# Where GpSimd computes the low part of the attention output, and where the two row maxima of a score tile lie

## The chip, the cores and the metric

The kernel is one program on one core of a Trainium2 chip. The metric is the device time of one execution in microseconds. Before the change three runs took 513.75, 514.60 and 514.68 us; the median is 514.6 us. Engine names are those of the profile: PE is the matrix engine (PEld its weight loads), DVE is VectorE, ACT is ScalarE, POOL is GpSimd, SP is the engine that issues the DMAs.

## The reference

Causal attention over 2 batches, 12 heads, 448 positions and 64 dimensions feeds a gated projection, which feeds a second projection with a SoLU and a layer norm. All matrices are float32.

```
scores = q k^T / sqrt(64), masked above the diagonal
attn   = exp(scores - max(scores)) / (sum + 1e-9)
x      = attn v                      -> 896 tokens x 768
x      = (sigmoid(x w_gate) * (x w_val)) w_out       (768 -> 1536 -> 768)
h      = x w_in;  s = h * softmax(h);  out = layernorm(s) * g  w_out2   (768 -> 1024 -> 768)
```

## The kernel before

Each float32 operand is split into a high part that the matrix engine takes as it is and a low part (the operand minus its high part), and products are made from three terms: high x high, high x low, low x high. So every tensor that reaches PE has a "hi" instruction and a "lo" instruction.

The attention stage works on 12 pairs of heads. A table of steps, `STEPS` (lines 486 to 501), lists every operation with a step number and an engine; pair p does an operation of number s0 in step 8p + s0. In each step the loop at line 510 writes out, in this order, PE's operations, ACT's, DVE's and POOL's, and within an engine those of one step stand in the order of the table. So the table alone sets the order of each engine's instructions, and up to four pairs are under way at once. Each engine runs its own list in order and waits on semaphores.

The names that the change and the prediction use, with the step number in brackets:

- `sc_mm` (0 and 4; lines 319 to 339): the scores of a pair, in two groups of query tiles (448 + 64 keys, then 320 + 192 keys), into a PSUM tile `s`. The second group is the one that line L338 shows as 64x320.
- `sc_max` (0, 1, 4, 5; DVE, L351): the negated row maxima of a query tile for both heads of the pair, two numbers per partition, into columns 8 to 15 of a small tile `sum`. A maximum is named here by the columns that it reads over both heads: 896, 640, 384 or 128.
- `sc_exp` (1, 2, 5, 6; ACT, L358): exponentials with the maximum as bias, the row sums into columns 0 to 7 of `sum`.
- `sums` (7, POOL, L363, tile `rs`), `recips` (8, DVE, L367): the sums and their reciprocals. `rs_wide` (8, POOL, L374 through the helper at L221, tile `rx`): the reciprocals spread to 64 columns for each head. `rs_mm` (10, PE, L381, tile `r`): `rx` transposed on PE.
- `tr_mm`, `tr_hi`, `tr_lo` (from 9 on; PE L409, ACT L416, DVE L229, tiles `t` and `pt`): the exponentials transposed and split. `pv_mm` (13 to 20, PE L441): the products with v, tile `x`.
- `x_mul`, `x_hi`, `x_lo` (21, 22, 23; DVE L447, ACT L219, POOL L456 through L229; tiles `xf` and `xy`): the product times the reciprocals, and its two parts.
- for later pairs: `prep_k_hi` and `prep_q_hi` (-7 and -6, POOL L221 and L234), `prep_k_lo` (-5, DVE L229) and `prep_q_lo` (-2, DVE L249), all into `qks`; `prep_v_hi` and `prep_v_lo` (7 and 9, POOL L221 and L229, tile `v`); `last_keys` (3, POOL L221, tile `p`).

After the attention, from about 129.5 us on, come the matmuls of the two projections, with their weights streamed in and split.

Of the kernel before, what the change touches and what calls it, by code (L numbers as in the profile page):

```python
# [16 lines left out]
AX = mybir.AxisListType  # L17
PSUM = bass.MemoryType.PSUM

B, H, S, D = 2, 12, 448, 64  # L20
# [3 lines left out]
NQ = 4  # L24
# [20 lines left out]
def attn_moe_moe2(ctx: ExitStack, tc: tile.TileContext, qk, v, w_gv, w_out, w_in2, w_out2, g_ln, out):  # L45
# [3 lines left out]
    nc = tc.nc  # L49
# [140 lines left out]
    with ExitStack() as actx:  # L190
# [35 lines left out]
        ENG = dict(rx='P', qh='P', kh='P', kl='D', vh='P', vl='P', xh='A', xl='P', rr='A', lk='P')  # L226
# [65 lines left out]
        sum_t = [one.tile([128, 16], F32, name=f"sum{i}") for i in range(3)]  # L292
# [11 lines left out]
        ps = ps_x.tile([128, S], F32, tag="x", name="warm")  # L304
# [34 lines left out]
                                         rhs=t[rows, ck, :n], start=False, stop=(m == 2), skip_group_check=True)  # L339

        def sums_of(p, i, e):
            k = NQ * (1 - e) + i
            return sum_t[p % 3][:, k:k + 1], sum_t[p % 3][:, 8 + k:9 + k]

        def sc_max(p, i):
            ps = ps_sc[p, i]
            if p == 0 and i == GROUPS[0][0]:
                for e in range(2):
                    nc.vector.reduce_max(out=sums_of(p, i, e)[1], in_=ps[:, 1 - e], axis=AX.X, negate=True)
            else:  # L350
                nc.vector.reduce_max(out=sum_t[p % 3][:, 8 + i:16:NQ], in_=ps, axis=AX.X, negate=True)  # L351

        def sc_exp(p, i):
            n = QE[i]
            ps = ps_sc.pop((p, i))
            for e in range(2):
                sm, mx = sums_of(p, i, e)
                nc.scalar.activation(out=p_t[(2 * p + e) % NPB][:, POFF[i]:POFF[i] + n], in_=ps[:, 1 - e], func=AF.Exp,  # L358
                                     bias=mx, scale=1.0, accum_out=sm)
# [101 lines left out]
        def early_tiles():  # L461
# [31 lines left out]
            (-7, ENG['kh'], prep_k_hi), (-6, ENG['qh'], prep_q_hi), (-5, ENG['kl'], prep_k_lo), (-2, 'D', prep_q_lo),  # L493
            (3, ENG['lk'], last_keys), (7, ENG['vh'], prep_v_hi), (9, ENG['vl'], prep_v_lo),
            (7, 'P', sums), (8, 'D', recips), (8, ENG['rx'], rs_wide), (11, ENG['rr'], rs_out),
            (21, 'D', x_mul), (22, ENG['xh'], x_hi), (23, ENG['xl'], x_lo),
            (1, 'A', lambda p: sc_exp(p, 3)), (2, 'A', lambda p: sc_exp(p, 0)),
            (5, 'A', lambda p: sc_exp(p, 2)), (6, 'A', lambda p: sc_exp(p, 1)),
            (0, 'D', lambda p: sc_max(p, 3)), (1, 'D', lambda p: sc_max(p, 0)),
            (4, 'D', lambda p: sc_max(p, 2)), (5, 'D', lambda p: sc_max(p, 1)),  # L500
        )

# [7 lines left out]
        for s in range(PER * NPR + 26):  # L510
# [12 lines left out]
            for c in range(2 * NE + 2):  # L523
                e = s - 88 - 9 * c
# [32 lines left out]
    with tc.tile_pool(name="psg", bufs=8, space=PSUM, reuse_waits="tile") as psg:  # L557
        for t in range(NF):
            bs = (1,) if t < NE else (0, 1)
            ps = {}  # L560
# [29 lines left out]
    for m in range(NK):  # L590
        pm = php.tile([128, B, 512], F32, tag="h", name="pm")
        ps = [pm[:, b, :S] for b in range(B)]
# [170 lines left out]
```

## Time and profile before

| what | us |
|---|---|
| median of three runs | 514.6 |
| the three runs | 513.75 to 514.68 |
| span of the profiled execution, first to last instruction | 512.5 |
| PE busy in it | 501.2 |
| attention stage, to the first matmul of the gated projection | 129.5 |
| distance from one pair's `rs` to the next one's, pairs 2 to 9 | 8.7 |

The profile is of one execution, on the one core. Its span is what the instructions cover; a run's time holds some 2 us more that lie around the span. Times below are counted from the start of the span.

### The profile page before, as it was taken

The numbers are of one execution on the slowest core, as the hardware profiler recorded it, in microseconds if no ns is written. First come the engines' busy times: TensorE is split into PE (matmuls) and PEld (weight loads), VectorE is DVE, ScalarE is ACT, GpSimd is POOL, SyncE is SP. The second block draws the span as 40 slices with busy tenths as digits, with TensorE's granted clock in tenths as the row PEclk, the third lists the DMA queues.
The fourth block names the chain that finished last, engine by engine and source line by source line (L and its number), as shares of the span: only waits on it lengthen the run. The fifth ranks groups of instructions, "written<-read, shape, count | busy, mean of one in ns | idle before, by whom it ended". The sixth has DMA issues, their size and how long they took to land.

```text
span 512.5 us, 7699 instructions
## 1 busy us (share of the span) xinstructions
PE 501.2 (98%) x2980; PEld 457.1 (89%) x2980; DVE 335.9 (66%) x512; ACT 226.4 (44%) x481; POOL 118.0 (23%) x203
## 2 busy tenths in 40 slices
PE   8899999989999999999999999999999999999997
PEld 8888888878899999999999999999998888899997
DVE  4578787887655777887777766766753887841210
ACT  4677777784532454345434432343324242432211
POOL 3375757552000000000000000000050587710000
PEclk9899999999999999999999999999999999999999
DMA  5632323112333154355433532354440221000101
GB/s 150 184 92 77 92 79 93 42 49 76 125 123 99 66 165 164 125 163 161 137 116 125 182 123 68 139 165 164 133 176 1 86 100 62 0 32 33 61 32 61
DMA packets 13204, 52.79 MB, mean 103 GB/s; under 512 B 1776, under 2 KB 2288, under 8 KB 13168
## 3 DMA queue, kind: packets, MB, share of 16 engines
q1 hardware_dynamic: 13168, 52.31, 31.4%
q8 instruction: 23, 0.38, 0.3%
q14 instruction: 13, 0.11, 0.1%
HBM read 49.55 MB, written 2.75 MB: 102 GB/s over the span
## 4 chain that ended last, share of the span: by engine, by line
PE 81%; DVE 6%; ACT 6%; POOL 5%; issue 1%; POOLq 0%; ACTq 0%
PE gv L574 33%; PE pm L604 17%; PE po L695 12%; PE h L634 11%; ACT p L358 4%; DVE sum L351 4%; POOL v L229 2%; DVE qks L229 2%; PE gv L473 1%; PE warm L308 1%; POOL rx L221 1%; PE tp L677 1%; PE x L441 1%; PE s L338 1%; PE t L409 1%
## 5 line engine op out<-in xcount | busy, mean ns | idle before, releaser
L574 PE MATMUL gv<-xy,hl 128*128 128x448 f32 x828 | 168.1, 365 | 0.6 <-ACT pre L478 0.6
L574 PEld LDWEIGHTS gv<-xy,hl 128*128 128x128 f32 x828 | 155.5, 188 | 13.2 <-ACT pre L478 1.0
L604 PE MATMUL pm<-g,hl 128*128 128x448 f32 x432 | 87.7, 365 | 0.0
L604 PEld LDWEIGHTS pm<-g,hl 128*128 128x128 f32 x432 | 81.2, 188 | 6.4
L621 POOL TENSOR_SCALAR t<-t,g_sb 128x768 f32<-128x768 f32 x8 | 9.0, 1123 | 248.1 <-PE pm L604 248.1
L134 DVE TENSOR_TENSOR hl<-t,hl 128x768 fp32r<-128x768 f32 x36 | 35.1, 975 | 40.2 <-ACT hl L131 38.4
L695 PE MATMUL po<-wo,lt 128*128 128x384 f32 x336 | 60.7, 340 | 0.0
L634 PE MATMUL h<-wi,xy 128*128 128x512 f32 x252 | 59.2, 395 | 0.0
L695 PEld LDWEIGHTS po<-wo,lt 128*128 128x128 f32 x336 | 58.7, 188 | 0.2 <-POOL wo L626 0.2
L358 ACT ACTIVATE p<-s,sum 128x448 f32<-128x448 f32 (+3 forms) x96 | 45.0, 478 | 29.9 <-DVE sum L351 14.9
L634 PEld LDWEIGHTS h<-wi,xy 128*128 128x128 f32 x252 | 47.2, 188 | 11.4
L120 DVE SCALAR_TENSOR_TENSOR t<-raw,t 128x768 int32<-128x768 int32 (+1 forms) x56 | 53.0, 946 | 1.7
L117 DVE SCALAR_TENSOR_TENSOR t<-raw,t 128x768 int32<-128x768 int32 (+1 forms) x56 | 52.6, 939 | 1.8
L441 PE MATMUL x<-pt,v 128*128 128x320 f32 (+3 forms) x252 | 53.5, 327 | 0.0
L112 ACT ACTIVATE raw<-raw 128x768 f32<-128x768 f32 (+1 forms) x56 | 47.9, 866 | 10.3 <-DMA raw<-in_wo_dram 6.0
L351 DVE TENSOR_REDUCE sum<-s 128x2 f32<-128x128 f32 (+3 forms) x47 | 31.6, 672 | 15.2 <-ACT p L358 13.4
L441 PEld LDWEIGHTS x<-pt,v 128*128 128x128 f32 x252 | 38.1, 190 | 2.0
L229 DVE TENSOR_TENSOR pt<-t,pt 128x512 fp32r<-128x512 f32 (+1 forms) x48 | 31.9, 667 | 3.8 <-ACT pt L416 3.8
L115 DVE TENSOR_SCALAR t<-raw 128x768 int32<-128x768 int32 (+1 forms) x56 | 30.6, 547 | 4.9 <-ACT raw L112 4.9
L171 DVE TENSOR_TENSOR lt<-tp,lt 128x512 fp32r<-128x512 f32 x14 | 9.7, 690 | 36.4 <-ACT lt L170 36.4
L131 ACT CAST hl<-t 128x768 fp32r<-128x768 f32 x36 | 30.0, 832 | 4.6 <-PE pm L604 4.2
L179 ACT ACTIVATE wk<-gv 128x448 f32<-128x448 f32 x23 | 11.3, 542 | 43.1 <-PE gv L574 43.1
(90 smaller groups left out, 542.7 us busy)
## 6 DMA issues: line engine op xcount, KB each, us to landing
raw<-in_gv_dram SPq DMA_DIRECT2D x24, 768.0 KB, 4.4
raw<-in_wo_dram SPq DMA_DIRECT2D x20, 768.0 KB, 4.3
raw<-in_wi_dram SPq DMA_DIRECT2D x12, 512.0 KB, 3.5
qkr<-in_qk_dram SPq DMA_DIRECT2D x22, 224.0 KB, 3.5
vr<-in_v_dram SPq DMA_DIRECT2D x12, 256.0 KB, 2.6
out_dram<-o SPq DMA_DIRECT2D x6, 384.0 KB, 2.3
qkr<-in_qk_dram SPq DMA_DIRECT2D x4, 112.0 KB, 2.7
out_dram<-o SPq DMA_DIRECT2D x2, 192.0 KB, 1.8
```

The source lines that it names most:

```text
L112: nc.scalar.activation(out=w1.bitcast(F32), in_=w1.bitcast(F32), func=AF.Copy, scale=2.0 ** -112)
L117: nc.vector.scalar_tensor_tensor(out=tt, in0=w1, scalar=-2 ** 31, in1=tt, op0=ALU.bitwise_and, op1=ALU.bitwise_or)
L120: nc.vector.scalar_tensor_tensor(out=tt, in0=w0, scalar=29, in1=tt, op0=ALU.logical_shift_right, op1=ALU.bitwise_or)
L134: nc.vector.tensor_tensor(out=lo, in0=t_t.pop(it), in1=f32(hi), op=ALU.subtract)
L229: (nc.gpsimd if eng == 'P' else nc.vector).tensor_tensor(out=out, in0=a, in1=b, op=ALU.subtract)
L351: nc.vector.reduce_max(out=sum_t[p % 3][:, 8 + i:16:NQ], in_=ps, axis=AX.X, negate=True)
L358: nc.scalar.activation(out=p_t[(2 * p + e) % NPB][:, POFF[i]:POFF[i] + n], in_=ps[:, 1 - e], func=AF.Exp, bias=mx, scale=1.0, accum_out=sm)
L441: nc.tensor.matmul(out=ps[:, 128 * j:], lhsT=l, rhs=pt_t[h][:, c, u, c0:c0 + S - 128 * j], start=(chunk == 0 and n == 0), stop=(chunk == 7 ...
L574: nc.tensor.matmul(out=ps[i, b], lhsT=w[:, a, cs], rhs=xy[kk][:, x, b * S:(b + 1) * S], start=(kk == 0 and a == 0 and x == 0), stop=(kk == ...
L604: nc.tensor.matmul(out=ps[b], lhsT=w[:, a, cs], rhs=g_t[kk][:, x, b * S:(b + 1) * S], start=(kk == 0 and a == 0 and x == 0), stop=(kk == N ...
L634: nc.tensor.matmul(out=h[:, n * 512:(n + 1) * 512], lhsT=xy[kk][:, a, tk], rhs=wi[n * NK + kk][:, c], start=(kk == 0 and i == 0), stop=(kk ...
L695: nc.tensor.matmul(out=ps[n], lhsT=lts[k // 4][:, a, k % 4], rhs=wo[k][:, c, cs], start=(k == 0 and i == 0), stop=(k == NF2 - 1 and i == 2))
```

## The change

The two maxima of a query tile, which lay four columns apart in `sum` (columns 8 + i and 12 + i), come to lie side by side (columns 8 + 2i and 9 + 2i). And `x_lo` gets step number 24 instead of 23. In a step whose number leaves 0 when divided by 8 the table has `rs_wide` ahead of `x_lo`, so on POOL the low part of pair p - 2 now stands behind the widened reciprocals of pair p.

```diff
         def sums_of(p, i, e):
-            k = NQ * (1 - e) + i
-            return sum_t[p % 3][:, k:k + 1], sum_t[p % 3][:, 8 + k:9 + k]
+            k, m = NQ * (1 - e) + i, 8 + 2 * i + (1 - e)
+            return sum_t[p % 3][:, k:k + 1], sum_t[p % 3][:, m:m + 1]
...
-                nc.vector.reduce_max(out=sum_t[p % 3][:, 8 + i:16:NQ], in_=ps, axis=AX.X, negate=True)
+                nc.vector.reduce_max(out=sum_t[p % 3][:, 8 + 2 * i:10 + 2 * i], in_=ps, axis=AX.X, negate=True)
...
-            (21, 'D', x_mul), (22, ENG['xh'], x_hi), (23, ENG['xl'], x_lo),
+            (21, 'D', x_mul), (22, ENG['xh'], x_hi), (24, ENG['xl'], x_lo),
```

POOL's list, at the first pair that has an `x_lo` beside it (pair 2; `rs` are the sums, `rx` the widened reciprocals, `xy` the output's low part, `qks` the next keys, `v` the values):

```order
 L221 TENSOR_SCALAR v_0_140<-vr_116 128x128 [waits PE_49]
 L363 TENSOR_SCALAR rs<-sum_144 128x8 [waits Activation_49]
-L229 TENSOR_TENSOR xy_75<-xf,xy_75 128x448 [waits DVE_49]
-L221 TENSOR_SCALAR rx<-rs 128x512 [waits DVE_49]
+L221 TENSOR_SCALAR rx<-rs 128x512 [waits DVE_49]
+L229 TENSOR_TENSOR xy_75<-xf,xy_75 128x448
 L221 TENSOR_SCALAR qks<-qkr 128x448 [waits DMAHW7_49,DMAHW0_49]
 L229 TENSOR_TENSOR v_0_138<-vr_116,v_0_138 128x3x2x64 [waits Pool_49]
```

The same two rows change places at pairs 2 to 11, ten times; the `x_lo` of the last two pairs stand alone, as before. The wait that `xy` had is covered by the later one of `rx`.

DVE's list is the same before and after, waits included. Here is one pair of it in the changed kernel (the reciprocal, the maximum of 896 columns, then two low parts `pt`, the low part of the keys `qks`, and the maximum of 640 columns, which waits for PE):

```order
L367 RECIPROCAL rs<-rs 128x8 [waits Pool_49]
L351 TENSOR_REDUCE sum_143<-s 128x2 [waits PE_49]
L229 TENSOR_TENSOR pt<-t,pt 128x512 [waits Activation_49]
L351 TENSOR_REDUCE sum_143<-s 128x2 [waits Activation_49]
L229 TENSOR_TENSOR pt<-t,pt 128x512 [waits DVE_49,Activation_49]
L229 TENSOR_TENSOR qks<-qkr,qks 128x448 [waits DMAHW3_49,DMAHW2_49,Pool_49]
L351 TENSOR_REDUCE sum_143<-s 128x2 [waits PE_49]
```

The second maximum (128 columns) waits for ACT, with neighbouring columns as with distant ones. PE's and ACT's lists are the same too.

## Rows read from the trace of the kernel before

**Rows 1.** The page's first part: PE's busy time, its share, its instructions.

```profile
PE 501.2 (98%) x2980; PEld 457.1 (89%) x2980; DVE 335.9 (66%) x512; ACT 226.4 (44%) x481; POOL 118.0 (23%) x203
```

**Rows 2.** Busy time by stretch (one pair; the projections): PE, PEld, DVE, ACT, POOL, granted clock, DMA.

```profile
59.30:68.04 8.74, 8.59 (x84) 7.58 (x80) 7.19 (x12) 6.64 (x23) 5.69 (x10) 1.00 0.32 84
129.50:512.50 383.00, 379.72 (x1904) 348.81 (x1904) 237.07 (x335) 137.99 (x204) 47.41 (x73) 1.00 0.32 107
```

**Rows 3.** The chain that ended last, one pair: start, us, what.

```profile
59.30 0.26 POOL rs L363
...
63.30 0.98 DVE qks L229
64.28 0.82 DVE sum L351
```

**Rows 4.** Timeline of PE, same pair: start, us, instruction, [idle before <-releaser].

```profile
60.39 0.51 PEld L441 LDWEIGHTS x<-pt,v 128*128 128x128 f32 x3
61.42 0.14 PEld L381 LDWEIGHTS r<-identx,rx 128*128 128x128 f32 x1 [0.53 <-POOL rx L221]
...
61.80 0.14 PEld L409 LDWEIGHTS t<-identx,p 128*128 128x128 f32 x1
...
63.20 1.02 PE L338 MATMUL s<-qks 64*128 64x320 f32 x12
```

**Rows 5.** Timeline of DVE, same pair.

```profile
59.71 1.04 DVE L351 TENSOR_REDUCE sum<-s 128x2 f32<-128x896 f32 x1
60.67 0.68 DVE L229 TENSOR_TENSOR pt<-t,pt 128x512 fp32r<-128x512 f32 x1
...
63.30 0.98 DVE L229 TENSOR_TENSOR qks<-qkr,qks 128x448 fp32r<-128x448 f32 x1
...
64.26 0.83 DVE L351 TENSOR_REDUCE sum<-s 128x2 f32<-128x640 f32 x1
```

**Rows 6.** Timeline of POOL, same pair.

```profile
59.64 1.14 POOL L229 TENSOR_TENSOR xy<-xf,xy 128x448 fp32r<-128x448 f32 x1
...
60.75 0.62 POOL L221 TENSOR_SCALAR rx<-rs 128x512 f32<-128x512 f32 x1
...
61.33 0.57 POOL L221 TENSOR_SCALAR qks<-qkr 128x448 fp32r<-128x448 f32 x1
...
61.86 1.42 POOL L229 TENSOR_TENSOR v<-vr,v 128x384 fp32r<-128x384 f32 x2
...
63.24 0.57 POOL L234 TENSOR_SCALAR qks<-qkr 128x448 fp32r<-128x448 f32 x1
```

**Rows 7.** Timeline of pair 1, which has no `x_lo` beside it.

```profile
24.64 0.26 POOL L363 TENSOR_SCALAR rs<-sum 128x8 f32<-128x8 f32 x1 [4.91 <-ACT p L358]
25.22 0.62 POOL L221 TENSOR_SCALAR rx<-rs 128x512 f32<-128x512 f32 x1 [0.32 <-DVE rs L367]
...
28.66 0.62 DVE L229 TENSOR_TENSOR qks<-qkr,qks 128x448 fp32r<-128x448 f32 x1
```

**Rows 8.** All DVE instructions of L229 on `qks`: ns min/median/max, first and last start.

```profile
L229 DVE TENSOR_TENSOR qks<-qkr,qks x12: 614/978/987, 4.8 to 98.2; 128x448 fp32r<-128x448 f32 x12
```

**Rows 9.** Timelines of the last two pairs, 10 and 11.

```profile
104.97 1.42 POOL L229 TENSOR_TENSOR v<-vr,v 128x384 fp32r<-128x384 f32 x2
106.06 0.75 DVE L115 TENSOR_SCALAR t<-raw 128x768 int32<-128x768 int32 x1
...
107.90 0.83 DVE L351 TENSOR_REDUCE sum<-s 128x2 f32<-128x640 f32 x1 [0.50 <-PE s L338]
...
112.55 1.15 POOL L229 TENSOR_TENSOR xy<-xf,xy 128x448 fp32r<-128x448 f32 x1
112.95 1.56 DVE L134 TENSOR_TENSOR hl<-t,hl 128x768 fp32r<-128x768 f32 x1 [0.24 <-ACT hl L131]
113.66 1.33 POOL L221 TENSOR_SCALAR rx<-rs 128x512 f32<-128x512 f32 x1
...
115.05 0.33 PE L381 MATMUL r<-identx,rx 128*128 128x128 f32 x1 [0.55 <-POOL rx L221]
```

## The prediction, written before the changed kernel ran

> **What bounds the kernel now.** I read the busy times first [rows 1], then the stretches [rows 2], then the chain that ended last [rows 3], then the timelines of one pair, engine by engine [rows 4 to 6].
>
> The busy share points at PE, with 98% [rows 1], and for the projections that is right: from 129.5 us on PE is busy for 379.7 of 383.0 us at the full clock [rows 2]. The change touches nothing there, so that part only starts earlier or later. In the attention stage PE's share is as high, but its weight loads fill only 7.58 of 8.74 us, and DVE, ACT and POOL have idle time too [rows 2]. No engine is full; a loop over engines sets the length of a pair. The chain goes round it: sums on POOL at 59.30, low part of the keys on DVE at 63.30, maximum of 640 columns at 64.28 [rows 3], then exponentials on ACT, and the next pair's sums 8.74 us after the first, at 68.04 [rows 2].
>
> The chain has only one predecessor at each step, so I ask what else that maximum waits for. By the order of DVE it waits for PE's scores. These end at 63.20 + 1.02 = 64.22, and the maximum starts at 64.26 [rows 4, 5]. On DVE, an instruction that waits for nothing starts some 0.08 before the recorded end of the one in front (at 60.67, where the maximum of 896 columns ends at 59.71 + 1.04 = 60.75 [rows 5]). The low part of the keys ends at 64.28 [rows 5], so without the wait for PE the maximum would have started at 64.20. Two paths thus end within 0.06 us of each other:
>
> - PE's: POOL does x's low part from 59.64 and only then the widened reciprocals from 60.75 [rows 6]. PE is through with the loads in front at 60.39 + 0.51 = 60.90, stands idle for 0.53 us and begins their transposes at 61.42 [rows 4]. All that stands behind in its queue is late, the scores too.
> - DVE's: the low part of the keys lasts 0.98 us [rows 5], where the shortest of its kind takes 0.61 [rows 8]. POOL's high part of the queries runs from 63.24 to 63.81 [rows 6], and the low part ends 0.47 us after that. The same instruction takes 0.62 us in pair 1, where no x_lo delays POOL [rows 7]. So it is being held up by POOL, and goes on when that POOL instruction is over.
>
> **The change part by part.** Two neighbouring columns instead of distant ones: 47 maxima with two results each. Reading 640 columns takes 0.83 us [rows 5], 1.3 ns each, so two results are worth 2.6 ns; between a gain and a loss of that size, 47 x 2.6 ns = 0.1 us either way. I take 0. No wait goes with it, as DVE's list shows.
>
> The swap on POOL, ten times. x_lo is one instruction with no DMA in it, and the widened reciprocals are all that it is moved past. In the pair with its sums at T: now x_lo starts at T + 0.34, rx at T + 1.45, the next keys at T + 2.03, v's low part at T + 2.56, the queries' high part at T + 3.94 [rows 3, 6]. Changed, rx has to wait for the reciprocal: in pair 1, which has that order, it starts 0.58 after the sums [rows 7]. It keeps POOL 0.58 (60.75 to 61.33) and x_lo 1.11 (59.64 to 60.75) [rows 6], so x_lo starts at T + 1.16, the keys at T + 2.27, v's low part at T + 2.80 with its end at T + 4.22, the queries at T + 4.18. All that stands behind the swap comes 0.24 later, since POOL idles for the reciprocal. The keys' high part is still done long before T + 4.00, when DVE wants it.
>
> PE's path: rx is ready at T + 1.2 instead of T + 2.07, before PE arrives (60.90 is T + 1.60), so the idle 0.53 goes. What is late next: the transposes behind it reuse a PSUM tile that DVE's low part `pt` frees at 60.67 + 0.68 = 61.35 [rows 5]; with 0.04 for the signal they move from 61.80 [rows 4] to about 61.39. The gain on this path is 0.41: scores end at T + 4.51.
>
> DVE's path: the keys' low part still arrives at T + 4.00. Then POOL is in v's low part, to T + 4.22. If DVE goes on as soon as that is over, it ends at 4.22 + 0.47 = T + 4.69, where now it is T + 4.98, and the queries' high part waits for DVE instead. That POOL lets DVE in between two instructions that stand back to back is seen in pair 11: DVE's hl, which began at 112.95 behind x_lo (to 113.70), ended at 114.51, 0.81 after x_lo, while rx, queued right behind, took 1.33 us for its usual 0.62 [rows 6, 9]. The maximum can start at T + 4.69 - 0.08 = T + 4.61; it was T + 4.96. Gain 0.35, and this is the later of the two paths. From the other side: if POOL's hold ended a little later, 0.30; if the low part met no hold at all, PE's path would decide, 0.41.
>
> The Trainium skill (Perfetto Trace Analysis, GPSIMD Instruction) says not to trust the reported span of a GpSimd instruction and to use the spacing of starts. By that rule v's low part is over when the queries' high part starts, at T + 4.18, the keys' low part ends at T + 4.65, and eight pairs give 0.3 us more than the sum below. I keep the ends, since DVE's hl ended at the time that they give.
>
> This pattern stands in pairs 2 to 9, eight times: the median of the keys' low part over the run is 978 ns [rows 8]. From the maximum to the next sums nothing changes: ACT and DVE work by turns there, and PE and POOL, both earlier or idle, are not waited for. Eight pairs: 8 x 0.35 = 2.8 us.
>
> Pair 10 has no keys to prepare. There the maximum waits 0.50 for PE alone [rows 9]. PE gains 0.41 as above, to 107.49. But v's low part on POOL ends 0.24 later, at 106.63 instead of 106.39, and DVE's L115, which ends 0.42 after it now (106.81), ends at 107.05; the low part behind it ends 0.6 later, and the maximum can start at about 107.54. Gain 0.36.
>
> Pair 11: rx starts 0.24 after x_lo's present start, at 112.79, and is over at 113.41. PE, idle for 0.55 before 115.05 [rows 9], can start the transposes at 114.50. DVE's hl, which PE needs next, ends 0.81 after rx, at 114.22, in time. Gain 0.55; x_lo then waits for hl, and v's low part comes later, but PE needs it only four steps on.
>
> The sum: 2.8 + 0.36 + 0.55 = 3.7 us. The span becomes 508.8 instead of 512.5; the median of the runs stands 2.1 us above the span, which I keep: 514.6 - 3.7 = 510.9 us.
>
> **The rivals.**
>
> *POOL keeps its turn (slower).* If POOL's next instruction gets ahead of the waiting DVE, the keys' low part waits for the queries' high part as now, but that ends at T + 4.18 + 0.57 = T + 4.75. The low part ends at T + 5.22, the maximum starts at T + 5.14, 0.18 later than now: 8 x 0.18 = 1.4 us lost. In pair 11 hl would wait for x_lo as well, and the 0.55 goes; pair 10 keeps its 0.36. Sum 1.1 us slower, 515.7. For it: now, too, the low part waits for exactly this POOL instruction, which starts 0.06 ahead of it [rows 5, 6]. Against: pair 11, where DVE came in between. It decides once the queries' high part starts reading before DVE is let in. The Trainium skill (SBUF — State Buffer, SBUF: two separate sides) has it that of the two engines the one that starts first holds the shared ports for its whole instruction, which also puts the waiting low part first; the starts in rows 5 and 6 agree so far.
>
> *Only PE's wait goes.* If the keys' low part ends where it does now, because its 0.98 us is not POOL's doing, the maximum can start at 64.20 instead of 64.26: 8 x 0.06 + 0.36 + 0.55 = 1.4 us, 513.2. For it: 0.98 us is the same in eight pairs. Against: 0.62 us in pair 1 [rows 7].
>
> *Nothing.* PE's queue is in order, and what it gains at one wait it may lose at the next, for `pt` or for the queries' parts that now come later: 514.6. For it: PE's slack is small, its weight loads alone take 7.58 of 8.74 us [rows 2]. Against: the path behind the wait is followed above to the maximum.
>
> **How the numbers follow.** The forecast gets 0.70, the slower rival 0.08, the wait alone 0.12, nothing 0.10. The forecast's own range: eight pairs at 0.30 to 0.41 (2.4 to 3.3), pair 10 at 0.2 to 0.5, pair 11 at 0.3 to 0.9, so 2.9 to 4.7 us, 509.9 to 511.7. Half a microsecond is what the three runs differ by to either side. To hold 8 in 10 the range reaches to the wait alone, 509.7 to 513.3, and leaves out nothing and slower. A measurement here tells 0.2%, 1 us, from no change. Faster by more: the forecast and two thirds of the wait alone, 0.78. Within: the rest of that and nothing, 0.14. Slower by more: 0.08.
>
> **What would show it.** In the changed profile rx starts 0.58 after the sums in every pair, and the idle time of PE before L381 is gone in pairs 2 to 11. The keys' low part lasts some 0.69 us instead of 0.98, and the queries' high part is the one drawn out, to about 0.9. The sums follow each other after 8.37 us in place of 8.72. If they come 8.9 apart and the keys' low part lasts 1.2, POOL kept its turn. If PE's idle time turns up before L409 or L338 instead, it is nothing. If the low part gets short and the distance stays, the loop is another one than mine, and the prediction is wrong in its first part.

## The result, and the profile after

| | before | after |
|---|---|---|
| median of the runs, us | 514.64 | 510.40 |
| the runs, us | 513.75 to 514.90 | 509.67 to 510.87 |
| span of the profiled execution, us | 512.5 | 507.9 |
| `rs` to `rs`, pairs 2 to 10, mean us | 8.73 | 8.40 |
| `rs` of pair 10 to `rs` of pair 11, us | 9.29 | 8.89 |
| `rs` of pair 11 to the first matmul of the gated projection, us | 17.28 | 16.51 |

The ratio of the times is 0.9918, with a 95% interval of 0.9904 to 0.9932: 4.2 us faster. Forecast were 510.9 us and a gain of 3.7.

The trace says where the gain lies. From the first pair that has an `x_lo` beside it (pair 2) to the projections it is 8 x 0.33 = 2.6 us in the pairs, 0.4 us in pair 10 and 0.8 us in pair 11, together 3.8 us. The projections last as long as before. The other 0.85 us between the two spans stands ahead of pair 2, where the change moves nothing: the `rs` of pair 2 starts at 33.13 and 32.28 us. In the kernels run for this study that moment lies anywhere from 32.1 to 33.7 us. What differs there is PE's granted clock, as one stretch shows (columns: start and end, length, then busy time of PE, PEld, DVE, ACT and POOL, granted clock as a share of full speed, DMA share, GB/s). Before, with a mean of 0.67, so in part at the lower of the two levels (1.2 of 2.4 GHz):

```profile
17.00:20.00 3.00, 3.00 (x25) 2.88 (x23) 1.09 (x3) 2.16 (x10) 2.57 (x6) 0.67 0.98 274
```

After, at the full clock:

```profile
17.00:20.00 3.00, 3.00 (x38) 2.86 (x35) 1.41 (x4) 2.81 (x11) 2.83 (x6) 1.00 0.93 263
```

The kernel before itself runs in both ways: of its 18 executions beside the first set of experiments, those with a mean clock of 1.000 have spans of 511.6 to 511.8 us and those with 0.997 spans of 512.1 to 513.0 us. So the comparison below goes by distances within the stage and not by spans.

One pair after, to be laid beside [rows 4 to 6]. Its sums `rs` start at T = 57.48 us; for [rows 4 to 6] T was 59.30. POOL first (timeline: start, us, instruction, and in brackets the idle time before it and what ended it):

```profile
57.48 0.25 POOL L363 TENSOR_SCALAR rs<-sum 128x8 f32<-128x8 f32 x1 [2.08 <-ACT p L358]
58.06 0.62 POOL L221 TENSOR_SCALAR rx<-rs 128x512 f32<-128x512 f32 x1 [0.32 <-DVE rs L367]
58.64 1.15 POOL L229 TENSOR_TENSOR xy<-xf,xy 128x448 fp32r<-128x448 f32 x1
59.76 0.57 POOL L221 TENSOR_SCALAR qks<-qkr 128x448 fp32r<-128x448 f32 x1
60.29 1.43 POOL L229 TENSOR_TENSOR v<-vr,v 128x384 fp32r<-128x384 f32 x2
61.69 0.94 POOL L234 TENSOR_SCALAR qks<-qkr 128x448 fp32r<-128x448 f32 x1
```

The widened reciprocals start at T + 0.58, x's low part behind them, and the queries' high part at T + 4.21 lasts 0.94 us, where it was 0.57. PE in the same pair:

```profile
58.52 0.50 PEld L441 LDWEIGHTS x<-pt,v 128*128 128x128 f32 x3
59.03 0.14 PEld L381 LDWEIGHTS r<-identx,rx 128*128 128x128 f32 x1
59.64 0.14 PEld L409 LDWEIGHTS t<-identx,p 128*128 128x128 f32 x1
...
60.99 1.02 PE L338 MATMUL s<-qks 64*128 64x320 f32 x12
```

The row of L381 has no bracket any more: PE goes from one load to the next. Its scores end at 62.01, T + 4.53. DVE in the same pair:

```profile
58.85 0.68 DVE L229 TENSOR_TENSOR pt<-t,pt 128x512 fp32r<-128x512 f32 x1
...
61.48 0.72 DVE L229 TENSOR_TENSOR qks<-qkr,qks 128x448 fp32r<-128x448 f32 x1
...
62.13 0.81 DVE L351 TENSOR_REDUCE sum<-s 128x2 f32<-128x640 f32 x1
```

The keys' low part comes at T + 4.00 as before and lasts 0.72 us instead of 0.98. The maximum starts at T + 4.65, which was T + 4.96 [rows 5]. It is 0.12 after PE's scores, and 0.07 before the recorded end of the low part: the place of an instruction that follows its forerunner and waits for nothing else.

The chain that ended last no longer changes engine in a pair. These are the pieces around the place where [rows 3] had POOL and DVE:

```profile
58.79 0.61 PE x L441 x3
59.40 0.44 PE r L381 x4
59.84 0.57 PE t L409 x5
60.41 0.41 PE x L441 x2
60.82 0.24 PE s L329 x4
61.06 0.95 PE s L338 x10
62.01 0.66 PE x L441 x4
```

And the stretches that answer to [rows 2], one pair and the projections:

```profile
57.48:65.88 8.40, 8.40 (x80) 7.65 (x78) 6.86 (x12) 6.63 (x23) 5.84 (x10) 1.00 0.31 88
124.85:507.90 383.05, 379.71 (x1904) 348.78 (x1904) 236.90 (x335) 137.86 (x204) 47.38 (x73) 1.00 0.32 107
```

PE's busy time fills the pair, 8.40 of 8.40 us, where it was 8.59 of 8.74 [rows 2]. The reader should be wary of that, since a busy PE may still be one that waits with work in its pipe; one experiment below is for it.

### The profile page after: what moved, and what is told of

It reads as the page before. It is cut to its first block, busy times and chain, and to the rows that moved or that the text cites. A ratio compares the mean times of both kernels' runs of the same rounds, so it can differ in the third digit from the quotient of the medians.

```text
span 507.9 us, 7699 instructions
## 1 busy us (share of the span) xinstructions
PE 498.5 (98%) x2980; PEld 456.9 (90%) x2980; DVE 333.2 (66%) x512; ACT 226.1 (45%) x481; POOL 119.6 (24%) x203
## 4 chain that ended last, share of the span: by engine, by line
PE 95%; DVE 2%; ACT 1%; issue 0%; POOL 0%; POOLq 0%; DVEq 0%; ACTq 0%
PE gv L574 33%; PE pm L604 17%; PE po L695 12%; PE h L634 12%; PE x L441 7%; PE t L409 5%; PE s L338 4%; PE gv L473 2%; PE tp L677 1%; PE warm L308 1%; PE r L381 1%; ACT p L358 1%; PE s L329 1%; DVE sum L351 1%; DVE pt L229 0%
## 5 line engine op out<-in xcount | busy, mean ns | idle before, releaser
L115 DVE TENSOR_SCALAR t<-raw 128x768 int32<-128x768 int32 (+1 forms) x56 | 30.9, 553 | 4.9 <-ACT raw L112 4.9
L229 DVE TENSOR_TENSOR pt<-t,pt 128x512 fp32r<-128x512 f32 (+1 forms) x48 | 31.9, 666 | 1.9 <-ACT pt L416 1.9
```

The source lines that it names most:

```text
L229: (nc.gpsimd if eng == 'P' else nc.vector).tensor_tensor(out=out, in0=a, in1=b, op=ALU.subtract)
```

## The experiments

My theory: two paths from the sums to the maximum of 640 columns end within 0.06 us of each other in the kernel before, PE's (which waits for `rx`) and DVE's (which is held by POOL), and the change shortens both. Its rivals: only one of the two matters, the columns matter, or PE is full. The changed kernel ran 4 times and the others 5 to 11 times, each beside runs of the kernel before, and the ratio is to those runs: four for the changed kernel, 21 for the columns alone and the two kernels with an extra product (median 514.22 us), 18 for the remaining four (median 514.01 us). So a median is not to be compared with the 514.64 of the first row alone. "Distance" is the mean from `rs` to `rs` over pairs 2 to 10, read from the timelines; the columns "pair 10" and "pair 11 on" are the two end pieces of the first table, and the last one is the mean duration of the low part of the keys.

| kernel | median us | ratio, 95% interval | distance | pair 10 | pair 11 on | keys' low part, ns |
|---|---|---|---|---|---|---|
| before | 514.64 | | 8.73 | 9.29 | 17.28 | 981 |
| after | 510.40 | 0.9904 to 0.9932 | 8.40 | 8.89 | 16.51 | 718 |
| swap alone | 510.32 | 0.9913 to 0.9938 | 8.40 | 8.87 | 16.51 | 720 |
| columns alone | 514.16 | 0.9986 to 1.0004 | 8.75 | 9.32 | 17.29 | 990 |
| hold kept | 512.83 | 0.9965 to 0.9987 | 8.70 | 8.89 | 16.54 | 1020 |
| wait kept | 514.56 | 0.9993 to 1.0012 | 8.73 | 9.30 | 17.28 | 616 |
| late x_lo | 510.53 | 0.9914 to 0.9942 | 8.37 | 8.92 | 16.51 | 615 |
| extra product, before | 514.41 | 0.9995 to 1.0013 | 8.75 | 9.28 | 17.29 | 989 |
| extra product, after | 512.12 | 0.9949 to 0.9974 | 8.58 | 9.13 | 16.73 | 715 |

**The swap alone**, on the kernel before:

```diff
-            (21, 'D', x_mul), (22, ENG['xh'], x_hi), (23, ENG['xl'], x_lo),
+            (21, 'D', x_mul), (22, ENG['xh'], x_hi), (24, ENG['xl'], x_lo),
```

> The kernel before with x_lo's step number 24 alone; the maxima stay four columns apart. Two paths (mine): the columns are worth nothing, so the sums of pairs 2 to 9 follow each other after 8.40 us as in the changed kernel, the keys' low part lasts 0.72 us, and the time is 510.4 us. Rival, the columns bring part of it: the distance lies between 8.40 and 8.72 us and the time above 511.

510.32 us and 8.40 us from sums to sums: all of the gain (3.7 us against the 514.01 of the kernel before beside it). **The columns alone** are the rest of the change, with `x_lo` back at 23:

> The neighbouring columns alone, x_lo's step number 23 as before. Mine: nothing, the sums 8.72 us apart, 514.6 us. Rival, the columns bring part of the gain: below 514.

The ratio's interval holds 1 and the distance is that of before. The maxima themselves tell nothing apart either: that of 896 columns takes 1040 ns here and 1042 in the kernel before. The columns are worth nothing that these runs can show.

**POOL's hold kept, PE's wait gone**, on the changed kernel. x's low part goes where POOL is idle anyway, and a filler keeps the queries' high part at its old time:

```diff
-... (7, ENG['vh'], prep_v_hi), ...
+... (6, ENG['vh'], prep_v_hi), ...
-... (8, ENG['rx'], rs_wide), ...
+... (8, ENG['rx'], rs_wide), (8, 'P', filler), ...
-... (24, ENG['xl'], x_lo),
+... (30, ENG['xl'], x_lo),
...
+        fill_t = one.tile([128, 882], F32, name="fill")
...
+        def filler(p):
+            if 2 <= p <= 9:
+                nc.gpsimd.tensor_scalar(out=fill_t, in0=fill_t, scalar1=1.0, scalar2=1.0, op0=ALU.mult, op1=ALU.mult)
```

> The changed kernel without PE's wait but with POOL's hold as it was: x_lo goes behind the values' high part, where POOL is idle, and a filler of 882 columns on POOL behind the widened reciprocals puts the queries' high part back at T + 3.94 after the sums. Two paths (mine): the keys' low part takes 0.98 us again and decides alone, the maximum of 640 columns starts at T + 4.90, the sums come 8.66 us apart, and with the last two pairs' gain (1.2 us) the time is 512.9 us. Rival, PE alone (only PE's wait cost time, DVE's low part is hidden): 8.40 us apart, 510.4 us.

512.83 us, and 8.70 us from sums to sums. One pair with T = 58.20 (the helper's lines have moved by seven, so L388 is the transpose of `rx`):

```profile
59.71 0.14 PEld L388 LDWEIGHTS r<-identx,rx 128*128 128x128 f32 x1
...
61.71 1.02 PE L338 MATMUL s<-qks 64*128 64x320 f32 x12
62.17 0.57 POOL L234 TENSOR_SCALAR qks<-qkr 128x448 fp32r<-128x448 f32 x1
62.20 1.02 DVE L229 TENSOR_TENSOR qks<-qkr,qks 128x448 fp32r<-128x448 f32 x1
...
63.15 0.81 DVE L351 TENSOR_REDUCE sum<-s 128x2 f32<-128x640 f32 x1
```

PE waits for nothing at L388, its scores are ready at 62.73, and the maximum still starts only at 63.15, T + 4.95, when DVE is done. PE's wait removed alone is worth 0.02 us a pair. The filler overdid the hold a little: the queries' high part starts at T + 3.97, where it was T + 3.94 [rows 6], and the low part takes 1.02 us instead of 0.98. With the hold in its old place the maximum would have started some 0.04 earlier, so that the wait alone is worth up to 0.06 us a pair (an estimate from these rows). The gain of pairs 10 and 11, where there are no keys to prepare, is there but for 0.03 us.

**PE's wait kept, POOL's hold gone**, on the kernel before:

```diff
-(-6, ENG['qh'], prep_q_hi)
+(-4, ENG['qh'], prep_q_hi)
```

> The kernel before, with PE's wait for the widened reciprocals kept and POOL's hold taken away: the queries' high part is queued behind last_keys, so it no longer runs when DVE's low part of the keys comes. Two paths (mine): the low part falls to 0.62 to 0.75 us, PE still idles 0.53 us before L381, the maximum starts at T + 4.96 as before, the sums stay 8.72 us apart, 514.6 us. Rival, DVE alone (the chain of waits names only the low part): the sums come some 8.45 us apart and the time is 512.4 us.

514.56 us, 8.73 us from sums to sums. One pair with T = 59.58:

```profile
61.69 0.14 PEld L381 LDWEIGHTS r<-identx,rx 128*128 128x128 f32 x1 [0.53 <-POOL rx L221]
...
63.48 1.02 PE L338 MATMUL s<-qks 64*128 64x320 f32 x12
63.58 0.61 DVE L229 TENSOR_TENSOR qks<-qkr,qks 128x448 fp32r<-128x448 f32 x1
...
64.55 0.83 DVE L351 TENSOR_REDUCE sum<-s 128x2 f32<-128x640 f32 x1 [0.35 <-PE s L338]
```

The low part is over at 64.19, and DVE now idles 0.35 us for PE's scores. So the chain of [rows 3], which named the low part alone, was half of the story: shortening it by 0.36 us gained nothing. Together the two kernels show that either path alone held the old distance to within 0.02 us a pair.

**Neither left**, the changed kernel with x's low part behind the values' high part (the hold's diff without the filler):

> The changed kernel with x_lo behind the values' high part, where POOL is idle, so that neither PE's wait nor POOL's hold is left. Two paths (mine): the keys' low part takes 0.62 us, PE's scores end at T + 4.53 and now decide, the maximum starts at T + 4.57, the sums come 8.32 us apart in place of 8.40, 0.6 us less: 509.8 us. Rival, PE is full (the chain of the changed kernel is 95% PE): 8.40 us apart, 510.4 us.

Here the forecast missed. The low part falls to 615 ns, but the distance only to 8.37 us, between the two forecasts of 8.32 and 8.40, and the time is that of the changed kernel within the intervals. One pair, T = 58.82:

```profile
62.36 1.02 PE L338 MATMUL s<-qks 64*128 64x320 f32 x12
62.82 0.61 DVE L229 TENSOR_TENSOR qks<-qkr,qks 128x448 fp32r<-128x448 f32 x1
63.43 0.82 DVE L351 TENSOR_REDUCE sum<-s 128x2 f32<-128x640 f32 x1
```

PE's scores end at T + 4.56 instead of T + 4.53 and the maximum follows 0.05 later. With a shorter pair PE comes later into it, as if it had no time to give. The last pair of kernels asks for that with one more product per pair, just ahead of PE's transposes of `rx` (`CHUNKS` lists the products with v step by step, `TERMS` the three terms of each):

```diff
-... '00 00', '00', '10 10' ...
+... '00 00', '00 00', '10 10' ...
-iter(TERMS)
+iter(TERMS if a or j else TERMS + TERMS[2:])
```

> The kernel before with one more product per pair on PE, 448 columns wide, just ahead of the transposes of the widened reciprocals (one low term of the output is counted twice). PE needs 0.20 us for one such product (168.1 us for 828 of them in the projections). Both theories: PE idles 0.53 us there, so the product fits into the idle time, which falls to 0.33, and the sums stay 8.72 us apart; 514.6 us, 515.0 at most. If the distance grows by 0.2 us, PE was not waiting for POOL and the account of the kernel before is wrong.

> The changed kernel with the same extra product per pair. DVE's path decides (mine): PE has 0.1 us to spare before the maximum of 640 columns waits for it, so the sums come some 8.5 us apart in place of 8.40 and the time is 511.3 us. Rival, PE is full: every nanosecond of the product is paid, 0.20 us a pair, 8.58 to 8.60 us apart, and over twelve pairs 2.2 to 2.4 us more, 512.7 us.

In the kernel before the product is nearly free, 8.75 us for 8.73, and its place is in the wait, which fell from 0.53 [rows 4] to:

```profile
60.82 0.14 PEld L381 LDWEIGHTS r<-identx,rx 128*128 128x128 f32 x1 [0.32 <-POOL rx L221]
```

In the changed kernel it costs 0.18 us in each pair, 8.58 us for 8.40. Here, too, my forecast missed: the distance is the rival's (8.58 to 8.60) and not mine (8.5); the time, 512.12 us, lies between the two forecasts. The maximum now starts 0.05 after PE's scores, which end at 63.65, and no longer follows the keys' low part:

```profile
62.63 1.02 PE L338 MATMUL s<-qks 64*128 64x320 f32 x12
62.89 0.71 DVE L229 TENSOR_TENSOR qks<-qkr,qks 128x448 fp32r<-128x448 f32 x1
...
63.70 0.83 DVE L351 TENSOR_REDUCE sum<-s 128x2 f32<-128x640 f32 x1
```

One pair's stretch is again filled by PE (columns as in [rows 2]):

```profile
58.88:67.47 8.59, 8.59 (x84) 7.86 (x81) 6.95 (x12) 6.64 (x23) 5.84 (x10) 1.00 0.31 86
```

The waits between 30 and 104 us agree (in total, times, longest). Before, PE's weight loads wait for `rx`:

```profile
PEld r L381 <- POOL rx L221: 4.2, 8, 0.6
PEld L329 <- issue: 1.7, 8, 0.2
```

After, only the second kind is listed for PE and its weight loads:

```profile
PEld L329 <- issue: 1.9, 9, 0.2
```

So before, PE's busy share was partly waiting, and now it is work. The late `x_lo` gives that work's length, 8.37 us, and the changed kernel is 0.02 us a pair above it. The extra product says the same: of the 0.20 us that it needs, 0.02 fit in and 0.18 were paid. From this I conclude, without a run that tries all orders, that another order of POOL's list can bring no more than these 0.02 us in these pairs while PE's work stays as it is. No kernel that was tried is clearly faster than the changed one.

## Why the prediction was right

**The two paths.** I named them from a maximum that started 0.04 after PE's scores and 0.02 before the recorded end of the low part [rows 4, 5]. The two kernels that keep one path each confirm it to a few hundredths: 8.70 and 8.73 us where 8.66 and 8.72 were expected.

**PE's path.** A gain of 0.41 was forecast, scores ending at T + 4.51; it is T + 4.53, where it was T + 4.92 [rows 4]. The limit that I gave for it, the tile freed by `pt`, did not come into play: PE arrives at L409 at T + 2.16, when `pt` has ended at T + 2.05.

**DVE's path.** The step with the most risk, that DVE gets in between two POOL instructions that stand back to back, held in all eight pairs. The low part ends at T + 4.72 (forecast 4.69), the maximum starts at T + 4.65 (4.61), and the queries' high part takes 941 ns in the mean (0.9 forecast). The slower rival needed a low part of 1.2 us and there is none. The sum of the eight pairs is 2.6 us where 2.8 was forecast. The Trainium skill (Perfetto Trace Analysis, GPSIMD Engine Instruction) wants the spacing of starts used in place of GpSimd's reported spans. By that estimate the low part would have ended at T + 4.65; here the recorded ends were the better guide.

**Pair 10.** The gain was 0.40 us where 0.36 was forecast, by another way than I worked out, so that the nearness of the two figures is luck. v's low part is two instructions (384 and 128 columns), and DVE's L115 did not have to wait for both. It came shortly before the first one ended, at 102.73, took 0.57 us where it had taken 0.75 [rows 9], and the second one was drawn out from 0.46 to 0.78:

```profile
101.72 1.74 POOL L229 TENSOR_TENSOR v<-vr,v 128x384 fp32r<-128x384 f32 x2
...
102.57 0.57 DVE L115 TENSOR_SCALAR t<-raw 128x768 int32<-128x768 int32 x1
```

What the maximum waited for, 0.29 us, was still PE, whose scores end at T + 4.53 there too.

**Pair 11.** The gain was 0.77 us where 0.55 was forecast, the term that was most mis-sized. I took PE's idle time from the matmul row, 0.55 [rows 9], whose forerunner's end is modelled. PE's weight loads idled longer, and that is what came back:

```profile
115.04 0.14 PEld L381 LDWEIGHTS r<-identx,rx 128*128 128x128 f32 x1 [0.93 <-POOL rx L221]
```

That row is of the kernel before. After the change the load starts at 110.25, T + 1.91 in place of T + 2.82, and the chain from there to the projections is PE's but for two steps of ACT, as before. Of the 0.91 us by which the load came earlier 0.77 reached the projections; where the rest went I did not follow up.

**What I had wrong.** "No engine is full" holds for the kernel before, as the free extra product shows. But the reading behind it, weight loads that fill 7.58 of 8.74 us, was no measure of it: they fill 7.65 of 8.40 us where PE is full. For the changed kernel I compared only when two paths reach one maximum (gains of 0.35 and 0.41); that PE has little slack stood under a rival, without the amount of its work. That work, 8.37 us, allows 0.35 and not the 0.41 that I gave as the most. It did not show in the number, by luck, since the two limits lie 0.02 us apart.

The sum of the terms was 3.7 us, the trace gives 3.8 and the runs 4.2. That the sum came so close to the trace is in part luck: 0.2 us too much for the eight pairs and 0.2 too little for pair 11 cancel. The 0.4 us between the trace and the runs are within what the runs of one kernel differ by (513.75 to 514.90 before).

## What to carry to other kernels

Where an instruction starts a few hundredths of a microsecond after two different things end, both must be shortened: the chain of waits names one of them, and either alone gained next to nothing here. A POOL instruction moved in its queue moves all POOL instructions behind it, and it mattered here as much as the wait that was to go whether one of these held up a DVE instruction. To learn whether a busy PE is full, give it one more matmul and see whether the time grows; put it just ahead of the wait in question. Behind a wait, which no run here tried, I would expect it to cost time even on a PE that is not full. And before forecasting that a wait goes, ask how much work is left for the engine that no longer waits.

## What the runs showed of the hardware that was not expected

VectorE's low part of the keys was held by the GpSimd instruction that was running when it came, but by that one only: in all eight pairs it ended 0.47 to 0.49 us after that one and ahead of the next one in GpSimd's queue, whose recorded time grew from 568 to 941 ns, while its own fell from 981 to 718. Two groups of the changed kernel show it (mean ns behind the busy time):

```profile
L234 POOL TENSOR_SCALAR qks<-qkr 128x448 fp32r<-128x448 f32 x8 | 7.5, 941 | 0.0
...
L229 DVE TENSOR_TENSOR qks<-qkr,qks 128x448 fp32r<-128x448 f32 x8 | 5.7, 718 | 0.0
```

In pair 10 of the changed kernel the same happened with the two instructions of v's low part and L115 between them, and in pair 11 DVE's `hl` ended 0.80 us after `rx`, while `xy`, next in GpSimd's queue, took 1.85 us where it takes 1.15.

And the weight loads' idle time of some 0.22 us ahead of the mask's matmuls (L329), marked as issue, is there in every kernel, also where PE is full. It is no reserve: with it the extra product still cost 0.18 of its 0.20 us.
